# Letting score tiles, background products and prologue transposes take any of seven PSUM banks, with another order table

## The chip, the cores and the metric

The kernel runs on one core of a Trainium2 chip. The core has engines that run at the same time, each with its own in-order queue: TensorE (PE, matrix products, whose weight loads are shown as PEld), VectorE (DVE), ScalarE (ACT), GpSimd (POOL) and SyncE (SP, which here issues the DMAs). They meet only through semaphores. TensorE writes to PSUM, 8 banks of 128 partitions by 512 float32; ACT and DVE read results out of PSUM into SBUF. The metric is the device time of one execution in microseconds (us), lower is better.

## What is computed

The input x has 2048 rows of 640. It is layer-normalised to xn, which feeds two branches whose results are joined:

```
xn = layernorm(x)
s  = attention(xn)       # 32 heads of 20; softmax over 2048 keys; then @ wo
g  = silu(mlp(xn))       # gelu(layernorm @ w1), four shifted quarters, @ w2, residual,
                         # then gelu(layernorm @ w3) @ w4, residual
out = x + s * g
```

The attention has 32 x 2048 x 2048 = 134 million exponentials. That is the largest part of the work for ACT and DVE.

## The kernel before

**Tiling.** The heads go in 8 quads of four. A quad is cut into 4 query chunks of 512, and a chunk into 16 key tiles of 128. For one key tile and two heads the scores fill a *score tile*: 128 partitions by 1024 float32, which is two PSUM banks. ACT reads the tile with one exponential (L1432), writes bf16 to a buffer PT, and TensorE multiplies that with the values (L1233), adding up in PSUM bank 7, which belongs to these sums alone. Nine key tiles use a *wide* tile of four banks and one exponential of 2048 (L1414).

Some tiles have their exponential on DVE instead. `score_both` (task names `sb...`) makes two score tiles with one group of four matmuls: one goes to ACT, the other to DVE, which turns it into integers (L1459, tasks `u...`), makes shifted copies (L1358, tasks `s...`), and TensorE multiplies each with the values (L1367, tasks `pvd...`). If the two banks of DVE's tile are not neighbours, L1459 is two instructions of 512 in place of one of 1024.

**Two forms of a score product.** The four heads lie in four groups of 32 rows. In the row form (L1375) a head is one matmul on its 32 rows, and matmuls of different heads run side by side. In the column form (L1390) a head is four matmuls of 32 output columns against a masked copy of the queries (QM): 8 matmuls for a tile. A task `sc...` with a masked copy is flexible: it takes the row form if the task before it or after it on TensorE is a row-form or a flexible one, else the column form. So the order decides the form. `sr...` tasks make both tiles of a key tile at once in row form, `sb...` likewise.

**Background products.** Projections for later quads, the values, and the whole MLP branch are products through `mm_tile` (line L640): several tasks add into one bank of 128 by 512 or 320, and DVE reads it out (L1109, L1171, L1712, L1744, L1783, L1798, L1567). They are put between the score tasks on TensorE.

**Prologue and tail.** The rows of x are loaded, normalised on DVE, ACT and POOL, and transposed by TensorE (L963, tasks `tr_x...`) into xnT; the projections of the first four heads follow (`KT_`, `QA_`, `QT_`), a bound on the keys (L1036), and then the scores begin. At the end, `last_half` treats the last chunk in halves of 256 queries, and `finish_qc` multiplies by wo (tasks `wob...`), joins with the MLP branch (L1567, L1586), adds x (L1628) and stores.

**Banks.** Each task that opens a PSUM tile names a *kind* and takes one of that kind's bank sets: W (a background product, one bank), S (a score tile, a pair), SD (the two tiles of `score_both`), SR (the two of `sr`), SW (wide). Before the change S has the pairs 01 and 23 only; W has 4, 5, 6; DVE's tile of SD has mostly 45, 56 or 46. The prologue transposes use banks 0 to 3 in turn under fixed names, outside these kinds, and an empty task named `gate` on TensorE's queue stands between the last of them and the first score. A set is free when the reader of its last tile has ended: an exponential of ACT or a read-out of DVE.

**Order.** Nothing is scheduled on the chip. A string in the source (`TABLE`) lists all 5483 tasks in one order; two characters give a task's number and one more character per opened tile gives the bank set. `follow` reads it, appends each task to its engine's queue, and derives the semaphore waits. A task on an engine never overtakes an earlier one on the same engine. The model times in `follow` (`dma_bw`, `row_end`, `c_pool` and the like) only say what the search behind the table believed; they issue nothing.

Of the kernel before, what the change touches and what calls it, by code (L numbers as in the profile page):

```python
# [57 lines left out]
class Planner:  # L58
    def __init__(self):
# [14 lines left out]
        self.dma_bw = 223.0  # L74
        self.dma_lat0 = 1900.0
# [141 lines left out]
    def follow(self, table):  # L217
# [24 lines left out]
        while at < len(table):  # L242
# [7 lines left out]
            st = max(row_at + 6.0, row_end[t.part]) if e == "pe" and pe_mode and t.mode else eng_free[e]  # L250
# [27 lines left out]
            if e == "pe":  # L278
                if t.mode != pe_mode:
                    t.finish += self.mode_cost  # L280
                if t.mode:
                    row_at = t.finish - t.dur
                    row_end[t.part] = t.finish
                pe_mode = t.mode
# [169 lines left out]
class Cfg:  # L454
# [5 lines left out]
    def __init__(self, S=2048, D=640, H=32, F=1536):  # L460
# [26 lines left out]
        self.AHEAD = 2  # L487
        self.UNITS = ((),
# [3 lines left out]
                      ((0, 0, 2), (1, 1, 2), (3, 0, 2), (5, 1, 2)))  # L492
# [25 lines left out]
            [4, 3, 2, 4])  # L518

# [51 lines left out]
def c_pool(n, kind="ts"):  # L571
    return 150 + (1.1 if kind == "ts" else 2.4) * n


class Gen:
# [8 lines left out]
    def alloc(self, name, shape, dtype):  # L584
# [4 lines left out]
        off = self.pl.alloc(name, n * esz)  # L589
# [57 lines left out]
    def build(self, plan_only=False):  # L647
        nc, pl = self.nc, self.pl
        with contextlib.ExitStack() as es:
            ARENA = 212480  # L650
# [7 lines left out]
            pairs = [(0, [0, 1]), (0, [2, 3])]  # L658
            high = [(0, [4, 5]), (0, [5, 6]), (1, [4, 6])]
            third = [(1, x[1]) for x in high[:2]]  # L660
            pl.kind("W", "B", [(0, [4]), (0, [6]), (1, [5])])
            pl.kind("S", "B", pairs + (third if self.cfg.THIRD else []))
            pl.kind("SD", "B", [(r + q, x + y) for r, x in pairs for q, y in high]
                    + ([(3, pairs[0][1] + pairs[1][1]), (3, pairs[1][1] + pairs[0][1])] if self.cfg.FALL else []))
            pl.kind("SR", "B", [(r + q, x + y) for r, x in pairs for q, y in high[:2]]
                    + [(3, pairs[0][1] + pairs[1][1]), (3, pairs[1][1] + pairs[0][1])])
            pl.kind("SW", "B", [(0, [2, 3, 4, 5])])
            pl.hold = {"pe": self.cfg.HPE, "dve": self.cfg.HDVE}
            if self.cfg.SAVE:
                pl.saves = {"SD": "W", "SR": "W", "SW": "W"} if self.cfg.SAVE != 3 else {"SD": "W"}  # L670
                pl.reserve = self.cfg.RESERVE
                pl.hard = self.cfg.SAVE == 2
            pl.pool("PT", 7)
            pl.kind("PT", "PT", [(0 if i == 6 else 1, [i]) for i in range(7)])
            pl.kind("PT2", "PT", [(0, [i, i + 1]) for i in (0, 2, 4)])
# [1257 lines left out]
```

## Time and profile before

| what | value |
|---|---|
| time, three runs | 862.06, 863.00, 863.29 us; median 863.0 |
| span of the profiled execution, first to last instruction | 859.6 us |
| the profiled execution's own time beside its span | not listed; the three timed runs lie 2.5 to 3.7 us above the span |
| ACT busy | 815.5 us (95%), of it 788 exponentials of 1024: 733.1 us |
| PE busy | 800.6 us (93%), 14542 matmuls |
| DVE busy | 734.7 us (85%), 1031 instructions |
| first exponential of the scores starts, last one ends | 33.66 us, 848.57 us |

In a line of groups the page gives engine, operation, result <- operands with their shapes, the number of instructions, their busy time in us, the mean of one in ns, and after the second bar the idle time of the engine just before them with what ended it. Mean durations overlap where an engine pipelines, so busy time divided by the count (930 ns for an exponential) is the pace. A busy PE may still be blocked: a matmul shows as running while the next waits. In a timeline the brackets hold the idle time before the piece and its releaser.

### The profile page before, as it was taken

Reading aid. Unit: us, or ns where it says so; the run is one execution under the profiler, and the core shown is the slowest. Engines: PE = TensorE matmul, PEld = TensorE weight load, DVE = VectorE, ACT = ScalarE, POOL = GpSimd, SP = SyncE. Lnnn points to the kernel's source line nnn. Section 1 sums busy time; section 2 is a strip of 40 time slices with the busy share of each in tenths; the row PEclk is TensorE's granted clock in tenths of the full one; section 3 lists DMA queues with packets and bytes.
Section 4 is the critical chain, followed back from the end, with each engine's and each line's share of the span. In section 5 each row is a group of like instructions: output and inputs, shape, how many; then the busy total and the mean of one; then the engine's idle time right before and its main releaser. Section 6 shows DMA issues by size and latency. Waiting matters only on the chain.

```text
span 859.6 us, 31925 instructions
## 1 busy us (share of the span) xinstructions
PE 800.6 (93%) x14542; PEld 338.8 (39%) x14542; DVE 734.7 (85%) x1031; ACT 815.5 (95%) x854; POOL 39.3 (5%) x75
## 2 busy tenths in 40 slices
PE   7999999999899999999988999999997899989996
PEld 4443333334344433333433444343333343424464
DVE  7649999998998899999877999998995889987655
ACT  7799999999999999999999999999999999999994
POOL 5510000000000000000000000000000000000000
PEclk9999999999999999999999999999999999999998
DMA  7000533222110022311033011313211102041312
GB/s 230 18 16 24 137 97 89 90 66 65 25 40 16 18 50 55 79 44 46 11 94 92 14 51 27 81 36 89 50 32 47 34 13 54 13 123 33 116 57 95
DMA packets 74487, 50.83 MB, mean 59 GB/s; under 512 B 44768, under 2 KB 69552, under 8 KB 74352
## 3 DMA queue, kind: packets, MB, share of 16 engines
q1 hardware_dynamic: 74352, 48.79, 21.1%
q8 instruction: 115, 1.88, 0.9%
q14 instruction: 20, 0.16, 0.1%
HBM read 34.53 MB, written 10.17 MB: 52 GB/s over the span
## 4 chain that ended last, share of the span: by engine, by line
ACT 63%; PE 29%; DVE 7%; issue 1%; DMA 1%; SPq 0%; DVEq 0%
ACT arena L1432 57%; PE psum L640 10%; PE psum L1375 5%; PE psum L1390 4%; PE psum L1367 3%; PE psum L1233 3%; DVE arena L1459 2%; ACT arena L1787 2%; PE psum L1274 1%; ACT arena L1803 1%; DVE arena L1358 1%; ACT arena L1414 1%; ACT arena L1716 1%; DVE arena L852 1%; PE psum L963 1%
## 5 line engine op out<-in xcount | busy, mean ns | idle before, releaser
L1432 ACT ACTIVATE arena<-psum 128x1024 bf16<-128x1024 f32 x788 | 733.1, 1039 | 20.8 <-PE psum L1375 17.8
L640 PE MATMUL psum<-arena 128*32 128x320 bf16 (+1 forms) x5952 | 359.2, 335 | 0.6 <-DVE arena L1459 0.2
L1459 DVE TENSOR_SCALAR arena<-psum 128x1024 uint16<-128x1024 f32 (+1 forms) x243 | 263.7, 1094 | 31.8 <-PE psum L1375 30.5
L640 PEld LDWEIGHTS psum<-arena 128*32 128x32 bf16 x5952 | 148.8, 97 | 132.6 <-issue 31.2
L1375 PE MATMUL psum<-arena 32*128 32x512 bf16 x1384 | 165.6, 387 | 34.6 <-ACT arena L1432 24.2
L1358 DVE TENSOR_SCALAR arena<-arena 128x4096 uint16<-128x4096 uint16 (+1 forms) x174 | 194.7, 1142 | 2.9 <-PE psum L1367 1.8
L1390 PE MATMUL psum<-arena 128*32 128x512 bf16 x2400 | 182.7, 381 | 3.1 <-ACT arena L1432 2.1
L1233 PE MATMUL psum<-arena 128*22 128x512 bf16 x1552 | 148.9, 383 | 2.4 <-ACT arena L1432 2.0
L1367 PE MATMUL psum<-arena 128*22 128x512 bf16 x1728 | 146.2, 381 | 3.3 <-DVE arena L1358 3.1
L1375 PEld LDWEIGHTS psum<-arena 32*128 32x128 bf16 x1384 | 42.0, 91 | 179.5 <-ACT arena L1432 115.1
L1390 PEld LDWEIGHTS psum<-arena 128*32 128x32 bf16 x2400 | 46.1, 95 | 69.3 <-ACT arena L1432 57.7
L1367 PEld LDWEIGHTS psum<-arena 128*22 128x22 bf16 x1728 | 40.6, 91 | 53.6 <-issue 15.5
L1233 PEld LDWEIGHTS psum<-arena 128*22 128x22 bf16 x1552 | 38.8, 91 | 49.9 <-issue 18.6
L1109 DVE CAST arena<-psum 128x512 bf16<-128x512 f32 x40 | 27.0, 682 | 11.7 <-PE psum L640 11.4
L1783 DVE CAST arena<-psum 128x512 bf16<-128x512 f32 x48 | 32.7, 681 | 3.0 <-PE psum L640 2.5
L1567 DVE SCALAR_TENSOR_TENSOR arena<-psum,arena 128x320 bf16<-128x320 f32 x32 | 15.5, 489 | 22.5 <-PE psum L640 22.3
L1171 DVE CAST arena<-psum 128x320 bf16<-128x320 f32 x32 | 15.1, 486 | 16.2 <-PE psum L640 16.0
L852 DVE BATCH_NORM_STATS2 arena<-arena 128x6 f32<-128x320 bf16 x54 | 23.7, 477 | 3.2 <-DMA arena<-in_A_x_dram 3.1
L1480 DVE STREAM_TRANSPOSE arena<-psum 128x512 f32<-128x512 f32 x31 | 21.9, 708 | 1.7 <-PE psum L1367 1.2
L1490 DVE STREAM_TRANSPOSE arena<-arena 128x512 bf16<-128x512 bf16 x31 | 21.8, 702 | 0.2
L1744 DVE TENSOR_TENSOR arena<-psum,arena 128x320 bf16<-128x320 f32 x32 | 15.1, 480 | 7.2 <-PE psum L640 7.0
L1488 DVE TENSOR_TENSOR arena<-arena 128x512 bf16<-128x512 f32 x31 | 21.1, 680 | 0.1
(118 smaller groups left out, 364.2 us busy)
## 6 DMA issues: line engine op xcount, KB each, us to landing
arena<-in_B_w_dram SPq DMA_DIRECT2D x48, 160.0 KB, 2.6
arena<-arena SPq DMA_DIRECT2D x124, 32.0 KB, 2.2
arena<-in_B_w_dram SPq DMA_DIRECT2D x4, 960.0 KB, 5.7
arena<-in_A_x_dram SPq DMA_DIRECT2D x8, 320.0 KB, 5.9
arena<-in_A_x_dram SPq DMA_DIRECT2D x16, 160.0 KB, 2.3
out_dram<-arena SPq DMA_DIRECT2D x16, 160.0 KB, 1.8
heads<-arena SPq DMA_DIRECT2D x112, 20.0 KB
arena<-keys SPq DMA_DIRECT2D x28, 80.0 KB
```

Source lines behind the costliest of these rows:

```text
L640: ins = e.matmul(pb[32 * c:32 * c + 32, 0:N], lhsT(k, c), rhs(k, c), start=(k == 0), stop=(stop and k == nk - 1), tile_position=(0, 32 * c))
L852: lambda e, li=li, n=n, hh=hh: e.bn_stats(st[:, li, 6 * hh:6 * hh + 6], xn[:, n, hD * hh:hD * hh + hD]),
L1109: T("dve", c_dve(512), lambda e, h=h, c=c: e.tensor_copy(KS[:, 512 * c:512 * c + 512], self.wbank(h)[:, 0:512]), reads=[wa], writes=[A("KS ...
L1233: ins = e.matmul(pb[32 * i:32 * i + 22, 0:512], VA[:, ql, kts[i // 2], i, :], PT[:, slots[i // 2][0].slot, 512 * (i % 2):512 * (i % 2) + 512],
L1358: T("dve", c_dve(w, "4x"), lambda e, v=v, dst=dst: e.tensor_scalar(dst, U[:, ub, 0:w], EXP_B[v], None, op0=ALU.add), reads=halves, writes= ...
L1367: ins = e.matmul(pb[32 * i:32 * i + 22, 0:512], wv, dst[:, at:at + 512].bitcast(BF16), start=first, stop=final, tile_position=(0, 32 * i))
L1375: return e.matmul(out, self.KT[32 * i:32 * i + 32, b, 128 * kt:128 * kt + 128], self.QT[32 * i:32 * i + 32, b, 512 * qc:512 * qc + 512], s ...
L1390: ins = e.matmul(out[32 * c:32 * c + 32, :], self.KT[:, b, 128 * kt + 32 * c:128 * kt + 32 * c + 32], self.QM[:, gb, 2 * a + jj, :], start ...
L1432: lambda e: e.activation(self.PT[:, hp.slot, :], self.psum[:, 512 * hs.slot:512 * hs.slot + 1024], AF.Exp, scale=cfg.scale),
L1459: ins = e.tensor_scalar(U[:, ub, 1024 * at + 512 * k:1024 * at + 512 * k + w], self.psum[:, 512 * hd.slots[k]:512 * hd.slots[k] + w], a_ex ...
L1480: T("dve", c_dve(512), lambda e: e.transpose(Ob[:, :], self.bank(self.PVB)[:, :]), writes=[("PV", 0), A("Ob")], name=f"ob{quad}_{qc}", cls ...
L1783: T("dve", c_dve(512), lambda e, h=h, fc=fc, i=i: e.tensor_copy(GT[:, i, fc, :], self.wbank(h)[:, 0:512]), reads=[wa], writes=at, name=f"g ...
```

## The change

- The bank sets are listed anew. S may take any of six neighbouring pairs (01, 23, 12, 34, 45, 56), W any of the seven banks, SD and SR any two disjoint pairs, SW four sets.
- The prologue transposes open W tiles like the background products, and the `gate` task goes.
- The order table is a new one. Task names, their engines and their number (5482 without `gate`) stay; their order on every queue and their banks differ.
- New switches that could move work to POOL (`PN`, `PG`, `P3`, `PC`, `PP`) are all off, a sixth entry of `UNITS` is not used, and the numbers of the model (`dma_bw`, `dma_lat0`, `c_pool`, `row_end`) are other ones. The SBUF arena grows by 352 bytes, and the small buffers of the third layer norm are aligned to 16 bytes rather than 64.

```diff
-            pairs = [(0, [0, 1]), (0, [2, 3])]
-            high = [(0, [4, 5]), (0, [5, 6]), (1, [4, 6])]
-            third = [(1, x[1]) for x in high[:2]]
-            pl.kind("W", "B", [(0, [4]), (0, [6]), (1, [5])])
-            pl.kind("S", "B", pairs + (third if self.cfg.THIRD else []))
...
-            pl.kind("SW", "B", [(0, [2, 3, 4, 5])])
...
+            pairs = [[i, i + 1] for i in (0, 2, 1, 3, 4, 5)]
+            pl.kind("W", "B", [(0, [4]), (0, [6]), (1, [5])] + [(3, [i]) for i in range(4)])
+            pl.kind("S", "B", [(2 * (k > 1), p) for k, p in enumerate(pairs)])
+            pl.kind("SD", "B", [(2 * (k > 1) + 2 * (y > x + 1), p + [x, y]) for k, p in enumerate(pairs) for x in range(6, -1, -1)
+                                for y in range(x + 1, 7) if x not in p and y not in p])
+            pl.kind("SR", "B", [(2 * (k > 1), p + q) for k, p in enumerate(pairs) for q in pairs if not set(p) & set(q)])
+            pl.kind("SW", "B", [(0, [2, 3, 4, 5]), (0, [0, 1, 2, 3]), (1, [1, 2, 3, 4]), (1, [3, 4, 5, 6])])
...
-        self.T("pe", 0, None, writes=[("S", b) for b in range(4)] + [("gate",)], name="gate")
...
-                b = bk % 4
+                h, wa = self.wtile()
...
-                        pb = self.bank(b, BF16)
+                        pb = self.wbank(h, BF16)
...
-                    T("pe", c_pe(4, 128), fn, reads=[A("xn", n), A("ident")], writes=[("S", b)], name=f"tr_x{g}_{kc}_{n}")
+                    T("pe", c_pe(4, 128), fn, reads=[A("xn", n), A("ident")], writes=[wa], name=f"tr_x{g}_{kc}_{n}",
+                      acq=("W", h) if bi == 0 else None, tile=h.id)
...
-                    reads=[("gate",), A("KT", b, kt // 4), A("QT", b, qc), A("QTa", b, qc)] + ([] if gb is None else [A("QM", gb)]),
+                    reads=[A("KT", b, kt // 4), A("QT", b, qc), A("QTa", b, qc)] + ([] if gb is None else [A("QM", gb)]),
...
-    r"###^#6#q#_#f#(#3$)#]#}#)#$#7#[$9#8$D$Z#c$O&p#9#`#:#a#;#d#%#<#0#b&q#=&o$#$*#>#e#~#?(m#&#,$$#@(n#/$+#'#A#*$%#-#B$&$,#C#+#2$'#D#1#.#s$($-#E#F#u#G#H#v#I#4"
...
+    r"$Z#^#%#f#q##$)#,#(&p#)#&#6#3#7$##8#}#9#:#$#;$O#<#~$$#'#*#=$*#>#?#]&q$%$&#r#s#@#A$'$($D%4%#v#u#w#t#x#y#_$+$,#[#h%*#$-#k#|$.#z#c$9#g$[#j#B#C$/#D#E#i#F#l"
...
```

What the two tables say, counted from their entries:

| counted from the order table | before | after |
|---|---|---|
| flexible score tiles in row form / column form | 164 / 300 | 241 / 223 |
| runs of neighbouring row-form tasks on TensorE | 305 | 351 |
| steps in these runs (tasks of different heads share a step) | 406 | 445 |
| DVE tiles on two banks that are not neighbours | 27 of 216 | 29 of 216 |
| score tasks whose banks are freed by the exponential just ahead of their own | 17 | 2 |
| the same with one ACT task between | 713 | 628 |
| with two or more between, or freed by DVE alone | 42 | 144 |
| score tasks that wait for at least one read-out by DVE | 230 | 307 |
| of these, single tiles of kind S | 11 | 104 |

## The prediction

> **What bounds the kernel now.** I read the page's busy times, then ACT's timeline for its gaps, then the waits, then the timeline of PE and the windows around the gaps.
>
> From the page: busy times, and the groups of the exponentials, of the row-form scores and of DVE's read-outs.
>
> ```profile
> PE 800.6 (93%) x14542; PEld 338.8 (39%) x14542; DVE 734.7 (85%) x1031; ACT 815.5 (95%) x854; POOL 39.3 (5%) x75
> ...
> L1432 ACT ACTIVATE arena<-psum 128x1024 bf16<-128x1024 f32 x788 | 733.1, 1039 | 20.8 <-PE psum L1375 17.8
> ...
> L1459 DVE TENSOR_SCALAR arena<-psum 128x1024 uint16<-128x1024 f32 (+1 forms) x243 | 263.7, 1094 | 31.8 <-PE psum L1375 30.5
> ...
> L1375 PE MATMUL psum<-arena 32*128 32x512 bf16 x1384 | 165.6, 387 | 34.6 <-ACT arena L1432 24.2
> ```
>
> ACT is nearest to full, and its exponentials are idle 20.8 us, nearly all behind row-form scores. Those in turn wait for ACT: a ring. The waits say it from the side of the weight loads:
>
> ```profile
> PEld psum L1375 <- ACT arena L1432: 115.1, 252, 1.4
> PEld psum L1390 <- ACT arena L1432: 57.7, 204, 1.9
> PEld psum L1375 <- DVE arena L1459: 40.6, 88, 1.6
> ```
>
> Then ACT's timeline (start, length, what, idle before it): gaps of half a microsecond between trains of exponentials.
>
> ```profile
> 103.98 5.61 ACT L1432 ACTIVATE arena<-psum 128x1024 bf16<-128x1024 f32 x6 [0.50 <-PE psum L1375]
> 110.53 7.66 ACT L1432 ACTIVATE arena<-psum 128x1024 bf16<-128x1024 f32 x8 [0.95 <-PE psum L1375]
> ```
>
> And the timeline of PE: prices of the two score forms, and a block inside a run of row-form tiles.
>
> ```profile
> 504.35 0.39 PE L1375 MATMUL psum<-arena 32*128 32x512 bf16 x4
> 504.99 0.39 PE L1375 MATMUL psum<-arena 32*128 32x512 bf16 x2 [0.25 <-ACT arena L1432]
> 505.31 0.41 PE L926 MATMUL psum<-arena 128*32 128x128 bf16 x16
> ...
> 512.71 0.61 PE L1390 MATMUL psum<-arena 128*32 128x512 bf16 x8
> 513.14 0.58 PE L640 MATMUL psum<-arena 128*32 128x320 bf16 x12
> ```
>
> A single row tile holds PE from 504.99 to 505.31, 0.32 us; a column tile from 512.71 to 513.14, 0.43. The four matmuls at 504.35 should free PE by 504.67, but the next tile starts at 504.99: its banks were still being read.
>
> From the first exponential (33.66) to the end of the last (848.57) are 814.9 us, of which ACT works 793.9, so 21.0 are gaps. ACT's instructions are the same after the change, so 793.9 is a floor for this stretch; ahead of it lie 33.7, behind it 11.0.
>
> **Part 1, gaps of ACT (21.0 us).** I set each gap of 0.1 us or more beside the start of its score task and the end of the read that freed that task's banks. In 13 gaps, 7.4 us, the score began within 0.26 us of an exponential's end; in 12, 4.2 us, of a DVE read's; in 21, 8.7 us, the banks had long been free and PE itself was late. The rest is crumbs.
>
> *Banks freed by ACT.* The typical price is 0.50: 0.06 from the end of the exponential to the score and 0.44 to the next exponential. It is paid where nothing stands on ACT between the two. The table has 17 such score tasks before and 2 after. 7.4 x 2/17 = 0.9, a gain of 6.5 (bounds 0 and 7.4).
>
> *Banks freed by DVE.* 230 score tasks need a read by DVE before, 307 after. At 4.2/230 = 18 ns each that is 5.6, a loss of 1.4. Bounds: a gain of 4.2 if spare pairs hide them all; a loss if all 93 additional single tiles stall at the mean of those gaps, 0.35 us, 32.8. I take the mean rate, since in most of the 230 an ACT task covers the read.
>
> *PE late.* Each run of row-form tasks costs about 0.105 to get in and out, and 0.216 a step (0.32 for one step, 0.54 for two, in runs without a block). Before: 305 x 0.105 + 406 x 0.216 + 300 columns x 0.432 = 249.3. After: 351 x 0.105 + 445 x 0.216 + 223 x 0.432 = 229.3. So 20.0 us of PE's work go, out of some 717 at such slots. Row-form runs take 176.4 us in the trace against 119.7 by the prices: 57 us in which PE stood in front of busy banks while all behind it waited. Both help late scores. I take half of 8.7, a gain of 4.4 (bounds 0 and 8.7): less work does not move a product that stands in the wrong place.
>
> Sum of part 1: -6.5 + 1.4 - 4.4 = -9.5 us. With every gap gone it would be -21.
>
> No other engine takes over by its work: in stages of 40 ACT tasks, with each task's own duration from the trace, ACT has the largest sum in all but one full stage before (DVE 40.6 against 37.9) and all but two after (38.5 against 37.8, 37.7 against 37.2). That excess, 1.2 us, is inside the 5.6.
>
> **Part 2, prologue (33.7 us).** The first score needs all four key projections. Their path is DVE's: norms, read-outs, L1036 for the last chunk, then the shift. Removing `gate` buys nothing: the transposes ahead of it feed those projections anyway. What moves: SP loads rows 2-3 second and 6-7 third. Before, DVE waited 1.09 us until 7.15 for the third load; now ACT waits instead, at most 1.6 us, and ACT is idle 2.35 us at 14.7 just after those statistics, which covers it; uncovered it costs 1.6. On POOL the last square root stands behind a norm of 0.87 us, so the last two norms can come 0.87 later. Two read-outs of 0.4 and one L1036 of 0.69 go behind those norms, 1.4 sooner. Key weights go behind rows 12-13, 115 KB and 400 KB more, some 2.5 us at 330 GB/s; all loads land by 17.5, and the first key product starts at 20.3. Two transposes now stand after the 11th warm-up task and wait for POOL's norm until about 7; warm-up products resume behind them, before PE's old idle stretch at 9.6 to 13.25. I take -1.0 (bounds -2.5 and +1.0).
>
> **Part 3, tail (11.0 us).** From ACT's last end at 848.57 to the transpose of the last half at 850.21 PE had nine products of wo and six value products. Now two value products follow the last exponential: 0.06 + 0.11 + 0.28 + 0.04 = 0.5 in place of 1.64.
>
> ```profile
> 850.21 0.45 DVE L1329 STREAM_TRANSPOSE arena<-psum 128x256 f32<-128x256 f32 x1
> 850.59 0.79 DVE L1586 SCALAR_TENSOR_TENSOR arena<-psum,arena 128x640 bf16<-128x640 f32 x1
> ...
> 853.65 0.44 DVE L1338 STREAM_TRANSPOSE arena<-arena 128x256 bf16<-128x256 bf16 x1
> 854.14 1.26 PE L1579 MATMUL psum<-arena 128*32 128x320 bf16 x16 [3.70 <-DVE arena L1338]
> ```
>
> Between those two transposes DVE ran joins and additions that the new order has ahead of or behind all four steps: 0.45 + 0.20 + 0.42 + 0.45 = 1.5. The last products start 2.05 after the last exponential instead of 5.57; a join of 0.8 may still be in the way: -3.2 (bounds 0 and -3.6).
>
> **Small edits.** Two more split reads by DVE: two halves last 1.36 us against 1.21 whole, +0.3 in sum, hidden by DVE's 31.8 us ahead of L1459; uncovered +0.3. Odd pairs cost nothing by themselves: DVE's read is 1.214 us on banks 56 and 1.212 on 45. Arena, alignment and model numbers issue nothing.
>
> Sum: -9.5 - 1.0 - 3.2 = -13.7; span 859.6 to 845.9. The profiled execution's own time isn't listed; the median of 863.0 is 3.4 over its span, so 849.3, say **849**.
>
> **The rivals.**
>
> *Every gap closes.* -20 rather than -9.5 in part 1: 838 to 839. For it: PE is 20 us lighter. Against: 628 score tasks still have just one exponential of 0.93 us to hide 0.5 in.
>
> *DVE sets the pace of single tiles, a small gain.* If some 20 of the 93 stall at 0.35, that is 7 us: 856.
>
> *DVE turns it into a loss.* From 40 stalls (14 us) it decides; at 60 it is 21.2 over the forecast's 849: about 870. Place: stages where DVE is over 95% busy, at 320 to 360 and 520 to 560. Behind a blocked score all of PE waits, the products that DVE is to read included. Against: DVE had 32 us of slack ahead of L1459.
>
> *The clock.* Three times, at 433, 669 and 771, the granted clock falls to half for 3.4 us; here is one (us, PE, PEld, DVE, ACT and POOL busy, granted clock, DMA):
>
> ```profile
> 664.00:668.00 4.00, 2.86 (x30) 0.71 (x26) 3.28 (x5) 4.00 (x5) 0.00 (x0) 1.00 0.00 0
> 668.00:672.00 4.00, 3.60 (x44) 1.47 (x48) 2.64 (x5) 3.33 (x5) 0.00 (x0) 0.62 0.36 110
> ```
>
> ACT loses 3.1 us at the three (0.33, 0.91, 0.68, 0.46, 0.34, 0.41), so 1.0 a fall. A lighter PE is idle more: eight more falls take back 8 us, 857. Against: the new blocks are short. The Trainium skill, TensorE: Matmul & The Clock Gate, HAM oscillation, says that idle stretches of over about 3.4 us halve the clock; here the window ahead of the fall still had PE 2.86 of 4 busy, so the trace shows it falling after less than a whole idle stretch. By that rule alone, none of the 0.3 us blocks would cost a fall, and the sum would stay 849.
>
> *It moves the wait only.* Gaps change place and tail and prologue drift back: 863.
>
> **How the numbers follow.** Forecast 0.62, its own range 842 to 855; every gap closed 0.05; DVE small 0.11; clock 0.07; no change 0.04; DVE loss 0.11. Within 0.2% (1.7 us, about what a measurement here can tell) is only the no-change case. Faster: 0.62 + 0.05 + 0.11 + 0.07 = 0.85; same 0.04; slower 0.11. The range leaves out the first 0.05, no change and the loss, 0.20: 840 to 861.
>
> **What would show it.** Counts: L1375 x1538, L1390 x1784, PE 14080, DVE 1033, L1459 x245. Idle before L1432 near 11 rather than 20.8; weight loads of L1375 waiting on ACT well below 115.1; those on DVE's L1459 above 40.6. First exponential near 32.7; last exponential to end near 7.8. Wrong would be: ACT gaps behind score tiles that DVE freed, many more windows with the clock near 0.6, or DVE idle before the first exponential.

## The result

The changed kernel takes 840.4 us (median of four runs, 840.0 to 842.6) against 862.8 for the kernel before, measured beside it. The ratio is 0.9745, interval 0.9730 to 0.9761: 22.4 us less, where 14 were forecast. The profiled execution took 840.3 us over a span of 838.6, so 1.7 us lie outside the span and not 3.4 as assumed; the span itself fell by 21.0.

From the page of the changed kernel: busy times, and the groups of the exponentials, of DVE's read-outs and of the row-form scores. L1432 is now L1439, L1459 is L1466, L1375 is L1382, L1390 is L1397, L640 is L654.

```profile
PE 787.4 (94%) x14080; PEld 329.4 (39%) x14080; DVE 739.5 (88%) x1033; ACT 812.9 (97%) x854; POOL 40.9 (5%) x75
...
L1439 ACT ACTIVATE arena<-psum 128x1024 bf16<-128x1024 f32 x788 | 731.5, 1048 | 10.5 <-PE psum L1382 6.1
...
L1466 DVE TENSOR_SCALAR arena<-psum 128x1024 uint16<-128x1024 f32 (+1 forms) x245 | 264.5, 1090 | 23.8 <-PE psum L1382 20.3
L1382 PE MATMUL psum<-arena 32*128 32x512 bf16 x1538 | 180.7, 385 | 31.9 <-ACT arena L1439 16.3
```

The idle time ahead of the exponentials is halved, 20.8 to 10.5 us, and that behind row-form scores fell from 17.8 to 6.1. DVE's read-outs wait less, too. Then three windows each, cut at the start of the first exponential and the end of the last (window, its length, busy time and instructions of PE, PE's weight loads, DVE, ACT and POOL, the granted clock, DMA share and GB/s). Before:

```profile
0.00:33.66 33.66, 28.02 (x676) 15.74 (x680) 24.69 (x89) 21.52 (x40) 15.77 (x44) 0.95 0.52 154
33.66:848.57 814.91, 769.47 (x13803) 321.25 (x13803) 702.64 (x928) 793.96 (x814) 23.50 (x32) 0.99 0.21 55
848.57:859.60 11.03, 3.13 (x78) 1.86 (x66) 7.39 (x15) 0.00 (x1) 0.00 (x0) 0.71 0.25 91
```

After:

```profile
0.00:29.60 29.60, 26.07 (x664) 13.90 (x668) 25.02 (x88) 21.09 (x40) 15.27 (x39) 1.00 0.51 147
29.60:831.26 801.66, 760.31 (x13400) 315.12 (x13392) 709.80 (x937) 791.77 (x814) 25.66 (x37) 0.99 0.22 57
831.26:838.60 7.34, 1.02 (x20) 0.43 (x20) 4.69 (x10) 0.00 (x0) 0.00 (x0) 0.85 0.25 91
```

So the prologue gave 4.1 us, the main stretch 13.25 and the tail 3.7. In the main stretch ACT's work is 791.8 in place of 794.0; the rest of the 13.25, 11.1 us, are gaps (21.0 to 9.9).

The waits of the row form's weight loads hardly moved (115.1 us on ACT and 40.6 on DVE before), so they were no measure of what the exponentials lose:

```profile
PEld psum L1382 <- ACT arena L1439: 117.3, 273, 0.8
PEld psum L1397 <- ACT arena L1439: 43.7, 151, 0.8
PEld psum L1382 <- DVE arena L1466: 37.8, 78, 0.9
```

### The profile page after: what moved, and what is told of

It reads as the page before. It is cut to its first block, busy times and chain, and to the rows that moved or that the text cites. A ratio compares the mean times of both kernels' runs of the same rounds, so it can differ in the third digit from the quotient of the medians.

```text
span 838.6 us, 31021 instructions
## 1 busy us (share of the span) xinstructions
PE 787.4 (94%) x14080; PEld 329.4 (39%) x14080; DVE 739.5 (88%) x1033; ACT 812.9 (97%) x854; POOL 40.9 (5%) x75
## 3 DMA queue, kind: packets, MB, share of 16 engines
q1 hardware_dynamic: 74352, 48.79, 21.6%
## 4 chain that ended last, share of the span: by engine, by line
ACT 71%; PE 19%; DVE 5%; DMA 2%; SPq 2%; issue 1%; DVEq 0%
ACT arena L1439 67%; PE psum L654 9%; PE psum L1382 2%; PE psum L1397 2%; PE psum L1374 2%; ACT arena L1421 2%; PE psum L1238 2%; PE psum L1279 1%; DMA arena<-in_A_x_dram 1%; ACT arena L1726 1%; ACT arena L1813 1%; DMA heads<-arena 1%; DVE arena L1466 1%; PE psum L967 1%; SPq L1135 1%
## 5 line engine op out<-in xcount | busy, mean ns | idle before, releaser
L1439 ACT ACTIVATE arena<-psum 128x1024 bf16<-128x1024 f32 x788 | 731.5, 1048 | 10.5 <-PE psum L1382 6.1
L654 PE MATMUL psum<-arena 128*32 128x320 bf16 (+1 forms) x5952 | 350.0, 336 | 1.9 <-ACT arena L1439 0.5
L1466 DVE TENSOR_SCALAR arena<-psum 128x1024 uint16<-128x1024 f32 (+1 forms) x245 | 264.5, 1090 | 23.8 <-PE psum L1382 20.3
L1382 PE MATMUL psum<-arena 32*128 32x512 bf16 x1538 | 180.7, 385 | 31.9 <-ACT arena L1439 16.3
L1365 DVE TENSOR_SCALAR arena<-arena 128x4096 uint16<-128x4096 uint16 (+1 forms) x174 | 196.7, 1145 | 2.9 <-PE psum L1374 1.7
L654 PEld LDWEIGHTS psum<-arena 128*32 128x32 bf16 x5952 | 146.1, 97 | 131.6 <-issue 37.8
L1374 PE MATMUL psum<-arena 128*22 128x512 bf16 x1728 | 152.3, 382 | 4.8 <-DVE arena L1365 4.8
L1238 PE MATMUL psum<-arena 128*22 128x512 bf16 x1552 | 147.5, 381 | 0.4
L1397 PE MATMUL psum<-arena 128*32 128x512 bf16 x1784 | 136.3, 382 | 2.1 <-ACT arena L1439 0.6
L1382 PEld LDWEIGHTS psum<-arena 32*128 32x128 bf16 x1538 | 47.4, 91 | 191.9 <-ACT arena L1439 117.3
L1397 PEld LDWEIGHTS psum<-arena 128*32 128x32 bf16 x1784 | 34.3, 95 | 54.1 <-ACT arena L1439 43.7
L1793 DVE CAST arena<-psum 128x512 bf16<-128x512 f32 x48 | 32.7, 680 | 1.5 <-PE psum L654 1.3
L1176 DVE CAST arena<-psum 128x320 bf16<-128x320 f32 x32 | 14.9, 488 | 15.2 <-PE psum L654 14.6
L865 POOL TENSOR_TENSOR arena<-arena 128x2 f32<-128x2 f32 (+2 forms) x10 | 9.0, 902 | 326.7 <-DVE arena L863 326.4
L1495 DVE TENSOR_TENSOR arena<-arena 128x512 bf16<-128x512 f32 x31 | 21.1, 681 | 1.7 <-DMA heads<-arena 1.5
```

Of the source, the lines that this page charges most:

```text
L654: ins = e.matmul(pb[32 * c:32 * c + 32, 0:N], lhsT(k, c), rhs(k, c), start=(k == 0), stop=(stop and k == nk - 1), tile_position=(0, 32 * c))
L1238: ins = e.matmul(pb[32 * i:32 * i + 22, 0:512], VA[:, ql, kts[i // 2], i, :], PT[:, slots[i // 2][0].slot, 512 * (i % 2):512 * (i % 2) + 512],
L1365: lambda e, v=v, dst=dst: e.tensor_scalar(dst, U[:, ub, 0:w], EXP_B[v], None, op0=ALU.add),
L1374: ins = e.matmul(pb[32 * i:32 * i + 22, 0:512], wv, dst[:, at:at + 512].bitcast(BF16), start=first, stop=final, tile_position=(0, 32 * i))
L1382: return e.matmul(out, self.KT[32 * i:32 * i + 32, b, 128 * kt:128 * kt + 128], self.QT[32 * i:32 * i + 32, b, 512 * qc:512 * qc + 512], s ...
L1397: ins = e.matmul(out[32 * c:32 * c + 32, :], self.KT[:, b, 128 * kt + 32 * c:128 * kt + 32 * c + 32], self.QM[:, gb, 2 * a + jj, :], start ...
```

## The experiments

Theory A comes from the prediction's first term: a tile that may take any bank waits less for one. Theory B: the new order and the lighter matrix engine do it. C and D came up on the way: in C the pace of the matrix engine makes the gaps, in D the gaps belong to the order as a whole.

All gaps below are idle time of 0.1 us or more just ahead of an exponential between the first and the last. I sort them by what PE did: either PE had paused for 80 ns or more within the 1.2 us before the exponential, or it had run on without a pause that the trace shows. The second case often means that the score tile simply stood too far back in the queue, but not always: the ends of matmuls are modelled, and a row tile that is shown as 0.39 us lets the next block start after 0.32, so a short pause is hidden. Of the 35 gaps of before in the last column, 13 (6.2 us) have a score tile that began within 0.26 us of the read that freed its banks.

| kernel | gaps | us | PE had paused | PE ran on |
|---|---|---|---|---|
| before | 45 | 19.7 | 10: 4.5 | 35: 15.2 |
| after | 19 | 9.2 | 4: 2.4 | 15: 6.8 |
| oldbanks | 231 | 153.8 | 161: 99.6 | 70: 54.2 |
| freebanks | 132 | 78.1 | 91: 56.8 | 41: 21.3 |
| freebanks2 | 46 | 21.1 | 10: 4.4 | 36: 16.7 |
| oldforms | 63 | 22.7 | 6: 2.9 | 57: 19.8 |
| lateforms | 39 | 11.4 | 5: 2.4 | 34: 9.0 |
| allrow | 22 | 8.8 | 3: 1.5 | 19: 7.3 |
| before_allrow | 51 | 22.3 | 9: 4.2 | 42: 18.1 |
| before_light | 40 | 17.9 | 11: 4.9 | 29: 13.0 |
| after_light | 25 | 10.3 | 7: 4.1 | 18: 6.2 |

Each row is one execution, the profiled one.

### oldbanks: the new order on the old bank sets

Entries of the order table, decoded (task, kind, banks); 541 of 1076 change:

```diff
-w1_0_3_0 W 2
+w1_0_3_0 W 4
-sr1_0_12 SR 34,56
+sr1_0_12 SR 23,56
-sc1_0_13_1 S 56
+sc1_0_13_1 S 23
```

> The changed kernel's order on every queue and its forms, but 541 tiles go back to a bank set of the old kind; the prologue and seven tiles keep the new sets, because in this order no old set is open for them. Theory A, the free choice of bank closes the gaps between the exponentials: the 13 us that the main stretch gained go, and since this order was laid out for free banks perhaps more, so 853 to 870 us, with the first exponential still at 29.6 and the tail still at 7.3. Theory B, the order and the matrix engine's lighter load (229 against 249 us on the tiles of both forms, by the prices of their groups) closed the gaps: 840 to 845 us.

Measured: 1016.6 us (1013.7 to 1016.9), ratio to before 1.178 (1.176 to 1.181), far outside both expectations.

```profile
L1439 ACT ACTIVATE arena<-psum 128x1024 bf16<-128x1024 f32 x788 | 753.6, 1028 | 155.2 <-PE psum L1382 79.8
...
L1382 PE MATMUL psum<-arena 32*128 32x512 bf16 x1538 | 197.7, 392 | 98.8 <-ACT arena L1439 83.4
```

The row-form products stand 83.4 us behind exponentials for their banks, against 16.3 after. With this deal of banks B falls. It proves neither A nor that the order is worth nothing by itself, for the old sets were dealt out by age alone, which also cost much in the old order (next run); another deal within them might lose less, and none was tried. The trace of the changed kernel does show that its order uses the freedom: of its 532 single score tiles, 236 take a pair that the old list lacks, and for only 21 of these was one of the two old pairs free when the tile started, with all other tiles left on their banks.

### freebanks: the old order, banks dealt out by age

```diff
-sc0_0_10_1 S 23
+sc0_0_10_1 S 01
-sc0_0_11_0 S 01
+sc0_0_11_0 S 23
```

> The order of before on every queue, but each of the 1076 flexible tiles takes the set of the new lists that has been free longest. Theory A: the main stretch shortens, by between the 9.5 us of the forecast and the 13.3 measured for the whole change, while the first exponential stays at 33.7 and the tail at 11.0, so 849 to 854 us. Theory B: nothing that matters, 861 to 864 us.

Measured: 933.8 us (931.3 to 935.1), ratio 1.083 (1.081 to 1.086). Both expectations missed, and A by its sign.

```profile
L1439 ACT ACTIVATE arena<-psum 128x1024 bf16<-128x1024 f32 x788 | 743.1, 1036 | 79.4 <-PE psum L1382 42.9
...
L1382 PE MATMUL psum<-arena 32*128 32x512 bf16 x1384 | 164.3, 387 | 66.0 <-ACT arena L1439 48.2
```

Here 91 of 132 gaps follow a pause of PE. In the trace 69 of these pauses end with an exponential, 22 with a read-out L1466 and none with the read-out of a background product. One explanation is that a background product in a bank of a score pair keeps the whole pair from the next score tile, which the old fixed partition had prevented; the run doesn't show it. Whether a better deal of free banks helps the old order is the question of freebanks2.

### oldforms: the new order and banks, the old forms

```diff
-                if t.flex and (pe_mode or (nx is not None and (nx.mode or nx.flex))):
+                if t.flex and t.name not in COLUMNS:    # the 300 tiles that were columns before
```

> The changed kernel's order and banks, but each flexible tile is computed in the form, row or column, that it had before. By the groups' prices this costs the matrix engine 33 us more (262 against 229 us). Theory A in its plain form, a free bank covers a matrix engine that is some us late: 840 to 843 us. Theory B, the lighter matrix engine is part of the gain: the 6 us of waits for the matrix engine that are left between exponentials grow back to the 17.8 of before or beyond, so 850 to 860 us.

Measured: 860.3 us (858.4 to 862.9), ratio 0.9975 (0.9961 to 0.9989). Of the 22 us only 2 are left.

```profile
L1409 PE MATMUL psum<-arena 32*128 32x512 bf16 x1384 | 168.6, 385 | 22.9 <-ACT arena L1466 10.7
...
L1424 PE MATMUL psum<-arena 128*32 128x512 bf16 x2400 | 176.7, 382 | 5.7 <-ACT arena L1466 3.8
```

(Lines are 27 further down here.) PE waits less for banks than after (10.7 against 16.3 in the row form), and yet the exponentials have 63 gaps, 57 of them with PE running on. I measured the load by slots: from the first matmul of a block to the first of the next block, pauses taken out, over the main stretch. Score slots are 281.9 us against 254.2, the others 503.5 against 505.6: 25.6 us more, and the stretch is 22.2 us longer in this execution (19.9 by the medians). In this order PE's added work is paid almost whole. That led to C.

### allrow: the new order and banks, all tiles in the row form

```diff
-                if t.flex and (pe_mode or (nx is not None and (nx.mode or nx.flex))):
+                if t.flex:
```

> The changed kernel with every flexible tile in the row form, 574 runs in place of 351 and no column tile; by the groups' prices 25 us less for the matrix engine (205 against 229). If the matrix engine's load still prices the gaps that are left (6.1 us behind its products), they halve: 836 to 838.5 us. If the gaps that are left are single events at fixed places (the stall at 33 us, clock falls), 839.5 to 841 us. If row tiles disturb whoever reads their banks, above 842.

Measured: 840.3 us (839.3 to 843.6), ratio 0.9752 (0.9726 to 0.9777): no change. The score slots fell from 254.2 to 228.3, but the others rose from 505.6 to 527.4: 4 us in all instead of 25. The price that I had for a row tile was wrong, as the next run shows most plainly.

### before_allrow: the kernel before, all tiles in the row form

The edit is the same as in allrow, made in the kernel before.

> The kernel before, with every flexible tile in the row form: its order and its banks as they were, the matrix engine lighter by 33 us (216 against 249 by the groups' prices). After the run oldforms, where 33 us more for the matrix engine cost 20 us, the question is whether its lightness alone gives the gain. If it does, the waits of the exponentials for products fall from 17.8 to below 10 and the time is 845 to 853 us. If the lightness is of use only where banks are free, because a row tile has to hold both its banks before it starts, 858 us to some us above 863.

Measured: 861.0 us (859.3 to 863.9), ratio 0.9984 (0.9967 to 1.0001). Score slots 275.8 to 242.4, a gain of 33.4; other slots 492.3 to 526.0, a loss of 33.7. The timeline of PE shows where. Before, two products of L640 between column tiles:

```profile
513.14 0.58 PE L640 MATMUL psum<-arena 128*32 128x320 bf16 x12
513.55 0.61 PE L1390 MATMUL psum<-arena 128*32 128x512 bf16 x8
...
514.20 0.45 PE L640 MATMUL psum<-arena 128*32 128x320 bf16 x8
514.47 0.61 PE L1390 MATMUL psum<-arena 128*32 128x512 bf16 x8
```

With all tiles in the row form, the same two:

```profile
513.96 0.59 PE L640 MATMUL psum<-arena 128*32 128x320 bf16 x12
514.48 0.39 PE L1375 MATMUL psum<-arena 32*128 32x512 bf16 x2
...
515.02 0.45 PE L640 MATMUL psum<-arena 128*32 128x320 bf16 x8
515.40 0.39 PE L1375 MATMUL psum<-arena 32*128 32x512 bf16 x2
```

Twelve matmuls hold PE for 0.41 us ahead of a column tile and 0.52 ahead of a row tile; eight, 0.27 and 0.38. So 0.11 us of each switch fall on the block ahead, and another 0.10 are in the row tile's own 0.32. A row tile alone costs 0.43 in all, just what a column tile costs; only several tiles in one run save anything. That PE stops when the form changes is also a rule of the Trainium skill, TensorEngine Tiling (Array Packing), Key Properties: a change of the tiling mode drains the engine; the trace agrees, with 0.21 us for in and out together. Since this kernel's PE was not lighter, the run says nothing on C.

### before_light and after_light: less work for PE

One step of each of 236 background products covers half its columns, so these kernels leave out part of those sums.

```diff
+                w = N // 2 if k == 2 and name[0] in "swv" else N
                 for c in range(4):
-                    ins = e.matmul(pb[32 * c:32 * c + 32, 0:N], lhsT(k, c), rhs(k, c), start=(k == 0), stop=(stop and k == nk - 1),
+                    ins = e.matmul(pb[32 * c:32 * c + 32, 0:w], lhsT(k, c), rhs(k, c)[:, 0:w], start=(k == 0), stop=(stop and k == nk - 1),
```

> The kernel before with its order, banks and forms, but in 236 background accumulations one step of each (four matmuls) covers half the columns, so part of those sums is left out; by the mean lengths of the groups (0.216 us for four of 512 columns, 0.135 for four of 320) this takes some 20 us from the matrix engine and nothing from the others. It is to price the matrix engine's load in the order of before, since the run before_allrow turned out not to lighten it: what its tiles saved (33.4 us of slots) the products behind them lost (33.7). Theory C, the matrix engine runs without pause and its pace makes the gaps (35 of the 45 gaps, 15.2 us, came when it had not paused for 1.2 us): 845 to 853 us. Theory A, the banks that a tile waits for make them: 860 to 863 us.

> The changed kernel with the same 944 matmuls of half width, which leaves the same part of the sums out, some 20 us less for the matrix engine. Of its 8.8 us of gaps above 0.1 us in the main stretch 6.8 came when the matrix engine had not paused for 1.2 us. If its pace makes what is left: 833 to 837 us. If what is left are the stall at 33 us, the clock's falls and the ScalarE's own work: 838 to 840.5 us.

Measured: before_light 859.9 us (857.7 to 861.5), ratio 0.9977 (0.9962 to 0.9991), so 1.4 to 2 us faster; after_light 838.1 (836.7 to 843.1), ratio 0.9725 (0.9705 to 0.9746), not told apart from the changed kernel. The other slots fell by 11.0 us in each rather than by 20, and the score slots rose by 2.4, so PE was some 8.6 us lighter. In the order of before the main stretch got 2.95 us shorter. In the new one it didn't (802.0 against 801.7), but the profiled execution took 4.9 us longer than the median of its kernel; by the medians the new order gained 2.3 us, but the intervals overlap. C in its plain form falls: in the new order a heavier PE costs nearly its whole load (oldforms), while a lighter one gives back a third of it at most in either order, as far as these runs tell.

The places of the gaps say why. Of the 45 gaps of before, 44 stand at the same exponential in before_allrow (19.4 us there, 18.9 here) and 37 in before_light (17.7 and 16.6), but only 7 in the changed kernel. Gaps that keep their place when PE's load changes speak for the order in which the products stand in the queue: theory D.

### lateforms: half of oldforms

Only the tiles of quads 4 to 7 go back to the old form, 152 of the 300:

```diff
+                early = t.name[:3] in ("sc0", "sc1", "sc2", "sc3")
-                if t.flex and (pe_mode or (nx is not None and (nx.mode or nx.flex))):
+                if t.flex and (t.name not in COLUMNS if not early else pe_mode or (nx is not None and (nx.mode or nx.flex))):
```

> As oldforms, but only the tiles of the later four of the eight groups of heads (152 of the 300) are put back into the column form they had before. Theory C, every us of matrix-engine time more is paid where it is added: the first half of the exponentials takes as long as in the changed kernel (399 us), the second about 12 us longer than its 402, and the time is 850 to 853 us. If the engine's reserve covers a half of the load: 841 to 846 us. If a few tiles of the early groups made the loss of oldforms: about 840 us.

Measured: 848.1 us (847.3 to 849.0), ratio 0.9837 (0.9819 to 0.9854), between two of the expectations. The first half of the exponentials took 397 us (after: 399), the second 411 (402). PE's slots are 8.8 us more (scores 254.2 to 266.9, others 505.6 to 501.7), the second half is 9 us longer; over the whole stretch it is 6.5. All 39 gaps of this kernel stand where oldforms has one. So the load is paid where it is added, nearly one for one in that half, and no few early tiles made oldforms slow.

### freebanks2: the old order, banks chosen with care

```diff
-v1_4_0 W 5
+v1_4_0 W 6
-sb2_0_2 SD 23,45
+sb2_0_2 SD 34,25
```

> The order of before again, with a gentler use of the free banks than in the run freebanks: 189 of the 1076 tiles take another set, 132 of them one that only the new lists have, each chosen so that by the lengths of the tasks in the queues no tile starts later than it did. Theory A, a tile that may take any bank starts earlier where it waited for one, would by the prediction's first term give up to 6.5 us back, so 855 to 860 us. Theory D, the gaps belong to the order (44 of the 45 of before stood at the same exponential in before_allrow, 37 in before_light, 7 in the changed kernel) and with all seven banks in use a choice among them adds none: 861 to 864 us, with the gaps where they were.

The minus lines in this diff are the banks that the table of before has. Measured: 863.05 us (862.3 to 864.6), ratio 1.0014 (1.0004 to 1.0025): no gain, rather a loss of 1.2 us.

```profile
L1439 ACT ACTIVATE arena<-psum 128x1024 bf16<-128x1024 f32 x788 | 733.6, 1038 | 22.3 <-PE psum L1382 16.9
...
L1382 PE MATMUL psum<-arena 32*128 32x512 bf16 x1384 | 166.0, 387 | 34.3 <-ACT arena L1439 23.0
```

Against 20.8 and 24.2 before, nothing moved, and 41 of the 45 gaps are in their old places. As a test of A the run is weaker than it looks. In before, 23 gaps (11.4 us) have a score task that began within 0.26 us of the read that freed its banks; in 18 of these the task has the same banks in freebanks2. The trace of before says why no other choice was made: for each of the 23, no set of the new lists, the tile's own included, came free more than 0.01 us sooner than the set it took, with the other tiles left on theirs. Most are the four-bank tasks `sb` and `sr`. So this is D against A in the old order: with that order a free choice for these tiles alone could not bring them forward, and in the new order 7 gaps of this kind, 3.1 us, are left.

### oldprologue and oldtail: the ends put back

```diff
-PE: warm10 tr_x1_3_4 tr_x1_1_4 warm11 warm12 ...
+PE: warm10 warm11 warm12 ...
-SP: ld_x4 ld_x2 ld_x6 ld_x0 ld_x14 ld_x8 ld_x10 ld_x12 ld_wp_0 ...
+SP: ld_x4 ld_x6 ld_x2 ld_x0 ld_x14 ld_x8 ld_x10 ld_wp_1 ld_x12 ...
```

> The changed kernel, but up to the first exponential every queue (matrix engine, DVE, ScalarE, GpSimd and the loads) has the order of before. If the prologue's 4 us come from that order, the first exponential starts at 33 to 34 again and the time is 843.5 to 845 us. If they come from the banks of the transposes, which keep their free choice here, it starts near 30 and the time is 840 to 841.5 us.

Measured: 842.2 us (839.7 to 847.5), ratio 0.9779 (0.9747 to 0.9810), between the two expectations and, by the intervals, not told apart from the changed kernel. In the profiled execution, one of 847.0 us, the first exponential starts at 32.64, 3.0 of the 4.1 us back. In the kernel that ran, 27 tiles of the prologue had the banks of before as well, the transposes among them, so the run doesn't part order from banks as its expectation had it. The windows from 9 to 14 us of before, after and oldprologue:

```profile
9.00:14.00 5.00, 1.36 (x32) 0.56 (x28) 5.00 (x22) 3.25 (x8) 3.35 (x6) 0.96 1.13 300
```

```profile
9.00:14.00 5.00, 4.20 (x116) 2.15 (x108) 5.00 (x22) 4.92 (x14) 3.45 (x5) 1.00 1.13 288
```

```profile
9.00:14.00 5.00, 1.94 (x52) 1.21 (x52) 4.87 (x21) 3.76 (x11) 3.54 (x7) 0.87 1.14 297
```

In the new order PE works here, on transposes that used to come later (4.20 us against 1.36 and 1.94), ACT gets its copies to do (4.92 against 3.25 and 3.76), and the clock stays whole: the granted clock falls to half for 3.4 us at 13.6 us before and at 12.7 here, and not in the prologue after. Each trace is one execution, and falls occur with either order; all traces together part the two roughly. With the new order and no fall the first exponential starts at 29.6 to 30.1 (after, oldtail, ve2later, allrow, oldforms, lateforms); with the new order and a fall at 13.3 and 13.7 us, at 32.1 and 32.0 (after_light, oldbanks). With the old order and a fall it starts at 32.6 to 34.2 (five kernels), and without one at 32.1 (freebanks2). So a fall goes with some 2 us in the new order (0.5 to 2.1 in the old), and the order is worth another 2 (0.5 to 2.5).

```diff
-PE: pv_h0_11 wob11_0_0 sh1_14 wob11_0_1 wob11_0_2 pv_h1_8 wob11_0_3 wob11_0_4 sh1_12 ...
+PE: pv_h0_11 sh1_14 pv_h1_8 sh1_12 wob11_1_0 wob11_1_1 wob11_1_2 sh1_15 pv_h1_9 sh1_11 wob11_1_3 ...
-DVE: on_h0 wobev11_0 wobev11_1 cmb11 wobev12 cmb12 wobev13 ob_h1 rz_h1 ...
+DVE: on_h0 wobev11_1 wobev11_0 cmb11 ob_h1 wobev12 cmb12 rz_h1 ...
```

> The changed kernel, but the end has the arrangement of before: nine products of the output weight's block 11 after the last score tile, blocks 12 and 13 later, and DVE's last fifteen tasks in the old order. If the tail's 3.7 us come from this arrangement, the last exponential to the end takes 10.5 to 11 us again and the time is 843.5 to 844.5 us. If they come from something else, such as how much DVE has left when the last exponential ends, 840 to 841.5 us.

Measured: 842.3 us (841.1 to 844.8), ratio 0.9772 (0.9748 to 0.9797); last exponential to the end 9.8 us instead of 7.3. Here are the last products of PE in the changed kernel and, in the second fence, in oldtail:

```profile
833.37 0.73 PE L1588 MATMUL psum<-arena 128*32 128x320 bf16 x16 [1.77 <-DVE arena L1343]
```

```profile
834.16 0.93 PE L1588 MATMUL psum<-arena 128*32 128x320 bf16 x16 [3.71 <-DVE arena L1343]
```

They wait 3.71 us for DVE's last transposition, as in the kernel before (3.70), against 1.77. So 2.5 of the tail's 3.7 us come from this arrangement; what gives the other 1.2 stays open. In the median the run lost 1.9, between the two expectations, and its interval overlaps that of the changed kernel.

### ve2later: a stall that the change brought

At 30 us the changed kernel has a new stall. First ACT's timeline with the two gaps, then DVE's and POOL's:

```profile
33.67 1.02 ACT L1439 ACTIVATE arena<-psum 128x1024 bf16<-128x1024 f32 x1 [0.92 <-PE psum L1382]
36.96 3.77 ACT L1439 ACTIVATE arena<-psum 128x1024 bf16<-128x1024 f32 x4 [2.26 <-PE psum L1382]
```

```profile
30.05 3.10 DVE L1672 TENSOR_SCALAR arena<-arena 128x16 f32<-128x16 f32 x1
30.56 2.60 DVE L1033 TENSOR_SCALAR arena<-psum,arena 128x512 bf16<-128x512 f32 x1
```

```profile
29.62 3.51 POOL L1052 MEMSET arena<- 128x4096 bf16 x1
```

Sixteen elements take DVE 3.10 us, until POOL's memset ends. The edit moves that one task, which nothing in the queue needs so early:

```diff
-DVE: aq0_2 ve2 qev_1 aq0_3 aq_3 vev0_2 vev0_1 qev_3 aq_2 qev_2 vev0_5
+DVE: aq0_2 qev_1 aq0_3 aq_3 vev0_2 vev0_1 qev_3 aq_2 qev_2 ve2 vev0_5
```

> The changed kernel with one DVE task of 16 elements moved behind the eviction that follows it, away from GpSimd's memset at 29.6 us; in the changed kernel's trace it took 3.10 us there, the eviction behind it 2.60, and the exponentials stopped for 0.92 and 2.26 us. If the memset slows whatever DVE does beside it, the eviction is slow in its place and the time stays at 840 to 841 us. If the tiny task alone is caught, the two gaps close and it is 837.5 to 839 us.

Measured: 839.55 us (835.3 to 840.1), ratio 0.9721 (0.9694 to 0.9748), between the two expectations. First ACT's timeline of it, then two pieces each of DVE's and POOL's:

```profile
30.07 1.94 ACT L1439 ACTIVATE arena<-psum 128x1024 bf16<-128x1024 f32 x2 [0.72 <-PE psum L1382]
32.19 1.94 ACT L1439 ACTIVATE arena<-psum 128x1024 bf16<-128x1024 f32 x2 [0.19 <-PE psum L1382]
34.38 8.62 ACT L1439 ACTIVATE arena<-psum 128x1024 bf16<-128x1024 f32 x9 [0.24 <-PE psum L1382]
```

```profile
31.02 0.81 DVE L1033 TENSOR_SCALAR arena<-psum,arena 128x512 bf16<-128x512 f32 x1 [0.42 <-PE psum L1022]
...
34.14 1.34 DVE L1014 TENSOR_SCALAR arena<-arena 128x512 uint16<-128x512 uint16 x1
```

```profile
30.09 3.51 POOL L1052 MEMSET arena<- 128x4096 bf16 x1
33.54 1.80 POOL L1053 MEMSET arena<- 128x2048 bf16 x1
```

The gaps of 0.92 and 2.26 us are gone, and the read-out L1033 takes 0.81 us beside the same memset. What is caught is TENSOR_SCALAR from SBUF to SBUF: L1014, elsewhere 0.28 us, takes 1.34 and ends at 35.48, just after the next memset (35.34), as the small task had ended at 33.15, just after the first (33.13). Not every SBUF instruction is: at 1.46 us in the changed kernel a TENSOR_REDUCE of 128x4 took 0.16 in the midst of a memset (1.37 to 2.62). The kernel before had such a catch too (L1009 at 41.97, 1.07 us), but no exponential waited for it. The time improves by about 1 us, which the intervals don't part from the changed kernel; of all the kernels run that compute everything it has the lowest median.

## Why the prediction came out as it did

The direction, the range (840 to 861) and the counts (L1382 x1538, L1397 x1784, PE 14080, DVE 1033, L1466 x245) hold. The time lies at the lower edge of the range and below the forecast's own part of it (842 to 855). The span fell by 21.0 us where 13.7 were summed; the missing 7.3 are, rounded, 1.6 from the gaps, 2.2 from ACT's own work, 3.1 from the prologue and 0.5 from the tail. Another 1.7 is the time outside the span, taken as 3.4 and found to be 1.7.

**Gaps, -9.5 forecast, -11.1 measured.** The sum is near, but one of its three terms has the wrong sign and another the wrong size. Here is the prediction's own cut, made again on both traces; it counts all 46 gaps of 0.1 us or more, one of a wide tile included, and on before it agrees with the prediction's to within two gaps.

| the score task began | before, gaps: us | after, gaps: us | forecast after, us |
|---|---|---|---|
| within 0.26 us of an exponential's end | 13: 7.4 | 2: 1.1 | 0.9 |
| within 0.26 us of a DVE read's end | 10: 4.0 | 5: 2.0 | 5.6 |
| later, its banks long free | 23: 8.9 | 12: 6.2 | 4.3 |

*Banks freed by ACT, -6.5*: right, 6.3 us went. The count of such score tasks in the tables (17 to 2) did foretell the count of gaps (13 to 2). It is a count of the new table, though, and so the work of order and banks together; no run shows free banks giving it alone. *Banks freed by DVE, +1.4*: wrong in sign, 2.0 us went. The rate of 18 ns for each score task that needs a read did not hold with 307 such tasks; one of the five gaps left, 0.9 us, is the stall of ve2later and waits for data and not for a bank. *PE late, -4.4*: 2.7 us went. What is left has another gap of that stall in it (2.26 us), which the prediction could not know. Its stated cause, 20 us less work, was mis-sized. The score slots did fall by 21.6 us (275.8 to 254.2), but the other slots rose by 13.3 (492.3 to 505.6), so PE's work fell by 8.3. The switch at the end of the block ahead, 0.11 us for each of 46 more runs, explains 5 of the 13.3; the rest stays open. Nor does less work by itself close such gaps (before_light: 8.6 us lighter, 2.95 us won). The sentence "less work does not move a product that stands in the wrong place" was right, and the halving that followed from it had nothing to stand on. That the errors of the last two terms, 3.4 and 1.7 us of opposite sign, partly cancel is luck.

What the runs put in its place: the main stretch's gain belongs to the new order together with the banks and the forms that it was laid out for. Take away the banks, with the old ones dealt out by age, and it is 1016.6 us; take away the forms, 860.3; give the banks to the old order, 863 or 934; lighten PE in the old order, 860. In none of these runs is a part worth its share alone, so the 13.25 us can't be divided among them. Which of the moves on PE's and DVE's queues close which gaps stays open; no run changed the order of the main stretch alone with free banks.

**ACT's own 793.9 us, "a floor".** It fell to 791.8 (windows above). In a train the exponentials overlap by some 0.1 us; this one, from ACT's timeline of the changed kernel, does 55 in 50.83, 0.924 each, where one alone takes 1.02:

```profile
42.69 50.83 ACT L1439 ACTIVATE arena<-psum 128x1024 bf16<-128x1024 f32 x55
```

Each gap breaks a train and costs that overlap on top of its idle time. With 26 gaps fewer that is some 2.6 us by this estimate; 2.2 were measured. oldbanks with its 231 gaps shows it from the other side: its stretch without the gaps is 816 us.

**Prologue, -1.0 forecast, -4.06 measured, outside its bounds (-2.5 to +1.0).** The step named DVE's path as the one that counts and then priced single moves on the other queues as delays. It missed that earlier transposes fill PE's empty stretch and feed ACT and DVE: from 3.8 to 27.9 us DVE is now busy 22.4 us instead of 19.75, and in the profiled execution the clock doesn't fall at 13.6 any more, which is worth some 2 us of the 4. That part is in some measure luck, since after_light and oldbanks have the same order and do fall. oldprologue gives 3.0 us back in its profiled execution, 1.8 in the median. The price of a fall, 1.0 us, had been read from the main stretch; ahead of the first exponential it is about twice that by the starts listed above.

**Tail, -3.2 forecast, -3.7 measured.** Right in mechanism and size: the last products were to start 2.05 us after the last exponential and start 2.11 after it; oldtail puts back 2.5.

**Small edits, 0.** Nothing in the traces speaks against it.

**The rivals.** "Every gap closes" named nearly this time (838 to 839), but half of the gaps are still there; prologue, tail and overlap made the difference. The two on DVE didn't come: four gaps, 1.1 us, are left behind tiles that DVE freed, and PE's weight loads wait 37.8 us for DVE where more than 40.6 was the sign. The clock fell twice in the main stretch instead of three times, at 34.2 us for 3.4 and at 634.9 for 6.8, which is the same 10.2 us at half clock. "It moves the wait only" is what freebanks2 does, a choice of banks without an order for it. Of the signs, idle time before the exponentials (10.5 for "near 11") and the tail (7.34 for 7.8) came. The first exponential (29.6 for "near 32.7") did not, nor did the weight loads' wait on ACT: "well below 115.1" is 117.3, while the matmuls' own wait there fell from 24.2 to 16.3. A likely reason is that it counts loads that stand ready early.

## What to carry to other kernels

In a kernel whose queues are laid out by hand, a freedom (any bank) is worth only what the order makes of it: test it both ways, old order with the new freedom and new order without, before a gain is put down to it. See whether gaps keep their places when a load changes; here those that did were not closed by saving work, while work added to the engine that feeds the bottleneck was paid almost whole. When a predicted term is judged, cut the new trace by the prediction's own rule, since another cut can give another verdict. And price a change of form on both of its sides, the block ahead included, and a gap with the overlap that it breaks.

## What the runs showed of the hardware

- The switch between the two score forms costs PE 0.21 us there and back, half of it at the end of the block ahead (0.52 against 0.41 us for the same twelve matmuls), so that a single row tile (0.32 by its own slot) is as dear as a column tile (0.43).
- A DVE instruction of 16 elements from SBUF to SBUF took 3.10 us beside a POOL memset of 3.51 us; away from it, at 39.87 us in ve2later, it took 0.17. The read-out from PSUM behind it ran in 0.81 beside the same memset once the small one was moved. The Trainium skill, GPSIMD Engine Reference, Specifications, says that POOL shares its SBUF interfaces with DVE and that they contend where a DVE instruction runs in a 2-port mode or has two SBUF inputs; the trace agrees with contention, but no run here shows in which mode the slow instructions ran.
- Half the columns in 944 background matmuls saved 11.0 us, 0.047 us for each group of four, where 0.108 and 0.067 were reckoned from the lengths of whole groups.
